# A fused attention and MLP kernel: the lower half of x behind the state update, chunks 8 to 11 in other places, and products of constants on TensorE among the first chunks

## The chip, the cores and the metric

The kernel runs on one core of a Trainium2 chip. The metric is the time of one execution on the device in microseconds; lower is better. The core's engines work side by side: TensorE (PE, with its weight loads shown apart as PEld), VectorE (DVE), ScalarE (ACT), GpSimd (POOL), and SyncE (SP), which here only issues DMA transfers. Every engine takes its instructions in the order in which the program lists them and waits for others through semaphores.

## The reference

Three layers in a row. The first is a linear attention with decay over blocks of 64 positions (batch 2, 8 heads, 768 positions, head size 64):

```python
for b in range(nb):
    intra = np.einsum('bhic,bhjc->bhij', qb, kb) * Dmask[None]
    intra = np.einsum('bhij,bhjd->bhid', intra, vb)
    inter = np.einsum('bhid,bhde->bhie', qb * lam_pow[None], kv_state)
    out[:, :, sl] = intra + inter
    kb_dec = kb * rev_pow[None]
    kv_state = lam_block[None, :, None, None] * kv_state + np.einsum('bhsd,bhse->bhde', kb_dec, vb)
```

Its output, 1536 tokens of 512 numbers, goes through `h = x @ w_in`, `g = max(0.01 h, h)`, `y = g @ w_out` (inner width 2048), and then through `((y @ w1) * (y @ w2)) @ w3 @ w_out` (width 1024).

## The kernel before

Tokens are worked in 12 chunks of 128 (two blocks of 64, all 8 heads); four chunks make a group of 512 tokens, three groups in all. Matrix products of the layers behind the attention are done with every float32 operand split into an upper and a lower half (a copy to `float32r` on ScalarE, and what is left by a subtraction on VectorE, line 161), three products for one.

`attention(n, rank, joined)` (line 350) lists the work of a chunk: two loads of 512 KB (q and k, then k and v; line 361), `k_decay` and `q_decay` (kd and qd), the front on TensorE (scores, then k times v for the new state; lines 369 to 381), the mask of the scores (line 384), for each of the two blocks a `fade` of the old state and an `update` (lines 441 to 462), and `outs`, the products of masked scores and of the state. Where `joined`, the outputs of the chunk before are laid between the products of this chunk's front in one operation (`scores`, line 420; recorded at line 429); this text calls such an operation a pass. `outputs` (line 513) issues the outputs of a group's last chunk alone (line 519). `done` (line 495) takes an output x from PSUM: `x_hi` on ScalarE, then the lower half on VectorE. The products of the attention are float32, 64 by 64 with 64 columns; two of them, or four in a pass, use different quarters of the array at once.

`unit_h` (line 556) makes one 128-wide piece of h for a group (12 products, line 530), `unit_y` (line 600) adds its share to y (12 products, line 537). They alternate; the first eight weight tiles serve all three groups before the next block of tiles is begun. Weights come as 64-bit numbers and are made float32 by ScalarE and VectorE (`convert`, line 213). All weight loads past the eighth stand in the program behind the outputs of chunk 7 (line 262).

The order of all this is not written out: `in_order` (line 64) simulates the engines with a cost for each operation in ns and, whenever an engine is free, lists the ready operation of the lowest `rank`. An operation is ready when what it comes `after` is done and its buffers are free; `behind` only asks that another has been listed. `RINGS` gives the number of buffers of each kind; those in `FIXED` are handed out in the order in which the program creates them. `PLACE` says which chunks load into `yf0`, `yf1`, `yf2` (memory that later holds y) instead of the two `inp` buffers; `CHUNKS` says beside which step k of the main loop a chunk is listed, with rank 100 + 20 k and a bit.

Of the kernel before, what the change touches and what calls it, by code (L numbers as in the profile page):

```python
# [14 lines left out]
P = 128  # L15
B, H, S, D = 2, 8, 768, 64
# [6 lines left out]
CPG = T // CH  # L23
# [99 lines left out]
def tile_kernel(ctx: ExitStack, tc, qkv, lamb, w_in, w_out, w1, w2, w3t, wo, out):  # L123
    nc = tc.nc
# [18 lines left out]
    def op(*args, **kwargs):  # L143
        o = Op(*args, **kwargs)
        ops.append(o)
        return o
# [3 lines left out]
    def new(buf, shape, dtype=F32):  # L150
        tags = TAGS.get(buf.ring, (buf.ring,))
        turn[buf.ring] = turn.get(buf.ring, -1) + 1
        buf.tile = pools[buf.ring].tile(shape, dtype, tag=tags[turn[buf.ring] % len(tags)], name=buf.ring)
        return buf.tile
# [4 lines left out]
    def lo(dst, hi_, src):  # L159
        def fn(e):  # L160
            engines[e].tensor_tensor(out=dst(), in0=src(), in1=hi_().bitcast(F32), op=ALU.subtract)  # L161
        return fn


    T_ = {}
# [170 lines left out]
    wo_buf, wo_first, wo_part = {}, {}, {}  # L336

    xs, x_ops = {}, {}
    st_op, x_done = {}, {}
    half = [slice(0, D), slice(D, P)]
    pend, turns = {}, []
# [4 lines left out]
    def attention(n, rank, joined):  # L350

        inp, a, qd, kd = Buf(PLACE.get(n, "inp")), Buf("a"), Buf("qd"), Buf("kd")
        sc, st = Buf("ps"), Buf("ps")
# [64 lines left out]
        back = pend.pop(n - 1) if joined else None  # L418

        def scores(e):  # L420
# [10 lines left out]
        fr = op(  # L431
            {"pe": 2100}, scores, rank, [*ld, k_op, *(back["after"] if back else [])],
            [sc, st, *(back["takes"] if back else [])], [inp, kd, *(back["uses"] if back else [])],
            behind=turns[-1:],
        )
        turns.append(fr)
        if back:
            back["done"](fr)
        masked = op({"dve": 660}, mask, rank, [fr, tables[0]], [a], [sc])

        def fade(k, c):
# [14 lines left out]
        def update(k, c, old):  # L456
            def fn(e):
                if old:
                    nc.vector.tensor_tensor(out=state(k), in0=st.tile[:, c], in1=T_["faded", c], op=ALU.add)
                else:  # L460
                    nc.vector.tensor_copy(state(k), st.tile[:, c])
            return fn

        for c in range(2 if carry else 1):
            k = 2 * n + c
# [3 lines left out]
                fo = op({"dve": 420} if early else {"act": 1000, "dve": 420, "pool": 700}, fade(k, c), rank + 0.4, [st_op[k], tables[1]], port=True)  # L469
            st_op[k + 1] = op({"dve": 420}, update(k + 1, c, old), rank + 0.5, [fr, fo, x_done.get(n - 2)], [], [st])  # L470

        g, c0 = divmod(n, CPG)
        px = Buf("acc" if early else "ps")
        if c0 == 0:
# [17 lines left out]
                            else:  # L492
                                yield o, state(2 * n + c)[h, p, :], qd.tile[h, p, c, :], False

        def done(xo):
            part = lambda v: xs[g].tile[:, v, :, c0 * CH : (c0 + 1) * CH]
            src = lambda: px.tile.rearrange("q p c i -> q p (c i)")
            r = xo.rank + 0.8

            def x_hi(e):  # L500
                nc.scalar.copy(part(0), src())  # L501

            o1 = op({"act": 580}, x_hi, r, [xo], [], [px, xs[g]])
            o2 = op({"dve": 660}, lo(lambda: part(1), lambda: part(0), src), r, [o1], [], [px, xs[g]])
            x_ops[g] += [o1, o2]
            x_done[n] = xo

        pend[n] = {
            "mms": outs, "done": done, "takes": [px, xs[g]] if c0 == 0 else [px], "uses": [inp, a, qd],
            "after": [masked, q_op, *([st_op[2 * n]] if inter else []), st_op[2 * n + 1]],  # L510
        }

    def outputs(n, rank):

        back = pend.pop(n)

        def fn(e):
            for o, w, mv, start in back["mms"]():
                nc.tensor.matmul(o, w, mv, start=start, stop=True, skip_group_check=True)

        xo = op({"pe": 2000}, fn, rank, back["after"], back["takes"], back["uses"], behind=turns[-1:])
        turns.append(xo)
        back["done"](xo)
# [32 lines left out]
    def unit_h(g, f, rank, rank_next):  # L556
        w, w_ops, wb = weight("in", f, g, rank)
        ps = Buf("ps")

        def mm(e):  # L560
            x = xs[g].tile
            full(new(ps, [P, T]), w, lambda b, cc: x[:, b, cc, :])

        def leaky(e):

            nc.scalar.activation(out=ps.tile, in_=ps.tile, func=AF.Prelu, alpha=0.01)  # L566

        o0 = op({"pe": 2720}, mm, rank, [*w_ops, *x_ops[g]], [ps], [wb, xs[g]], behind=last_h[-1:])
        last_h.append(o0)
        o1 = op({"act": 560}, leaky, rank_next, [o0], [], [ps])  # L570
        gp[g, f] = pair_ops(o1, ps, rank_next)
# [28 lines left out]
    def unit_y(g, f, rank):  # L600
        w, w_ops, wb = weight("out", f, g, rank)
        gb, g_ops = gp.pop((g, f))
        job = lambda c: (lambda v: w(v)[:, c * P : (c + 1) * P], lambda v: gb.tile[:, v, :])

        def evac(c, acc, o):
            if f < FB:
                def fn(e):
                    if c == 0:
                        yf[g] = const.tile([P, NCC, T], F32, tag=f"yf{g}", name=f"yf{g}")
                    nc.scalar.copy(yf[g][:, c, :], acc.tile)  # L610
                yf_ops[g, c] = op(
                    {"act": 560}, fn, rank + 1, [o, *([yf_ops[g, 0]] if c else [])], [] if c else [Buf(f"yf{g}")], [acc]
                )
            else:
                def fn(e):
                    nc.vector.tensor_tensor(out=yf[g][:, c, :], in0=acc.tile, in1=yf[g][:, c, :], op=ALU.add)
                yf_ops[g, c] = op({"dve": 660}, fn, rank + 1, [o, yf_ops[g, c]], [], [acc])
            if f == NF1 - 1:
                y_split(g, c, rank + 2)

        accumulate("y", g, f, FB, rank, [*w_ops, *g_ops], [wb, gb], job, EXACT, evac)
# [91 lines left out]


    consts = op({"dve": 100}, dve_consts, 0)
    lam_op = op({"q": 100}, load_lam, 0)
    pc = op({"pool": 600}, pool_consts, 0)
    tables = [
        op({"dve": 900}, table("dm", "w34_6", 0.0, lambda: T_["ident"][:, 0, :]), 0, [lam_op, pc]),
        op({"dve": 900}, table("lpow", "w34_7", 1.0, lambda: T_["zero"]), 1, [lam_op, pc]),  # L720
    ]
    PLACE = {0: "yf0", 1: "yf1", 2: "yf2", 5: "yf1", 6: "yf2", 9: "yf2"}
    for n in range(CPG):
        attention(n, 10 * n, n > 0)
    outputs(CPG - 1, 10 * CPG)
    rank = 100

    steps = [(g, f) for b in range(0, NF1, FB) for g in range(NG) for f in range(b, b + FB)]
    r = lambda k: rank + 20 * k
    CHUNKS = {0: (4, 5), 1: (6, 7), 2: (8,), 4: (9, 10), 5: (11,)}  # L730
    for k in range(2):
        unit_h(*steps[k], r(k - 2) + 10, r(k))
    for k, (g, f) in enumerate(steps):
        unit_y(g, f, r(k))
        for i, n in enumerate(CHUNKS.get(k, ())):
            attention(n, r(k) + 1 + 5 * i, n % CPG > 0)
            if n % CPG == CPG - 1:
                outputs(n, r(k) + 8)
        if k + 2 < len(steps):
            unit_h(*steps[k + 2], r(k) + 10, r(k + 2))  # L740
        if k >= len(steps) - 2 * NF2 and k % 2 == 0:
            wo_ops.extend(weight("wo", (k - len(steps) + 2 * NF2) // 2, 0, r(k) + 15)[1])
    rank = r(len(steps))
# [3 lines left out]
    for g in range(NG):  # L747
        r = lambda f: rank + 40 * f
# [7 lines left out]
        rank = r(NF2)  # L756
# [57 lines left out]
```

## Time and profile before

| | before |
|---|---|
| median of 3 runs | 560.65 us (560.33 to 561.94) |
| the profiled execution | 561.43 us |
| its span, first to last instruction | 559.7 us |
| TensorE busy | 540.2 us (97%) |
| VectorE busy | 316.0 us (56%) |
| ScalarE busy | 304.0 us (54%) |
| GpSimd busy | 68.9 us (12%) |
| moved by DMA | 54.07 MB, mean 97 GB/s |

All rows come from one profiled execution. Busy time of an engine says little by itself: what counts is where the engine that bounds a stage stands still, and what ended that. The timeline gives it in brackets behind an instruction: idle time before it, and the releaser. "issue" means that nothing in the profile explains the wait. The sums by stage give for each engine the busy time and, in brackets with an x, how many instruction records began there.

### The profile page before, as it was taken

How to read it: one execution, taken by the hardware profiler on the slowest of the kernel's cores; microseconds unless marked ns; L12 is line 12 of the kernel's file. 1: busy time of each engine (PE TensorE's matmuls, PEld its weight loads, DVE VectorE, ACT ScalarE, POOL GpSimd, SP SyncE). 2: the span in 40 equal slices, each digit the busy share in tenths (PEclk: the TensorE clock that was granted, in tenths of full speed). 3: DMA queues.
4: the chain of work that ended last, by engine and by line, in shares of the span. 5: the costliest groups of instructions: out<-in, count | busy, mean ns of one | idle time of the engine just before them, and what ended most of it. 6: DMA issues, size and time to landing. Idle time of an engine off the chain costs nothing.

```text
span 559.7 us, 9050 instructions
## 1 busy us (share of the span) xinstructions
PE 540.2 (97%) x3680; PEld 448.6 (80%) x3680; DVE 316.0 (56%) x519; ACT 304.0 (54%) x548; POOL 68.9 (12%) x60
## 2 busy tenths in 40 slices
PE   5699998999999999999999999999999999999997
PEld 4588886888888888888888888888888888888885
DVE  4797589781338951699816778884223333333331
ACT  4786797882228752486815666763334333343332
POOL 0033132000000000010101201110002111120110
PEclk9799999999999999999999999999999999999999
DMA  8971874541003440145501324420002000020002
GB/s 302 368 274 40 278 254 153 185 152 37 1 0 113 150 153 0 39 147 184 196 1 37 114 76 152 150 77 0 1 0 76 1 1 0 2 75 0 1 0 77
DMA packets 15738, 54.07 MB, mean 97 GB/s; under 512 B 1872, under 2 KB 1872, under 8 KB 15696
## 3 DMA queue, kind: packets, MB, share of 16 engines
q1 hardware_dynamic: 15696, 53.49, 27.5%
q8 instruction: 29, 0.48, 0.3%
q14 instruction: 13, 0.11, 0.1%
HBM read 50.33 MB, written 3.15 MB: 96 GB/s over the span
## 4 chain that ended last, share of the span: by engine, by line
PE 88%; ACT 4%; DMA 4%; DVE 2%; issue 1%; SPq 1%; ACTq 0%
PE ps L530 45%; PE acc L537 33%; PE ps L655 8%; DMA yf<-in_qkv_dram 2%; PE ps L429 1%; DMA inp<-in_qkv_dram 1%; PE acc L429 1%; ACT rn L235 1%; ACT rp L235 1%; ACT faded L447 1%; SPq L361 1%; ACT kd L399 0%; DVE f L254 0%; DVE rp L239 0%; ACT yf L610 0%
## 5 line engine op out<-in xcount | busy, mean ns | idle before, releaser
L530 PE MATMUL ps<-xy,wp 128*128 128x512 f32 x756 | 179.1, 389 | 0.0
L530 PEld LDWEIGHTS ps<-xy,wp 128*128 128x128 f32 x756 | 141.9, 188 | 29.6
L530 PE MATMUL ps<-xy,wa 128*128 128x512 f32 x396 | 95.3, 390 | 1.4 <-ACT xy L501 1.3
L537 PE MATMUL acc<-act,wa 128*128 128x512 f32 x396 | 96.1, 391 | 0.3 <-DVE act L161 0.3
L530 PEld LDWEIGHTS ps<-xy,wa 128*128 128x128 f32 x396 | 74.0, 188 | 17.3 <-ACT xy L501 1.4
L537 PEld LDWEIGHTS acc<-act,wa 128*128 128x128 f32 x396 | 73.9, 188 | 16.1 <-DVE act L161 0.7
L161 DVE TENSOR_TENSOR act<-ps,act 128x512 fp32r<-128x512 f32 x72 | 49.5, 687 | 60.2 <-ACT act L545 60.2
L537 PE MATMUL acc<-wp,act 128*128 128x512 f32 x288 | 69.0, 389 | 0.0
L235 ACT ACTIVATE rp<-raw,bp 128x512 f32<-128x512 uint16 x72 | 54.9, 766 | 19.1 <-DVE f L254 17.3
L157 ACT CAST wp<-wa 128x512 fp32r<-128x512 f32 x48 | 29.8, 622 | 64.5 <-PE ps L530 39.2
L537 PEld LDWEIGHTS acc<-wp,act 128*128 128x128 f32 x288 | 54.1, 188 | 11.2
L235 ACT ACTIVATE rn<-raw,bn 128x512 f32<-128x512 uint16 x72 | 54.5, 762 | 9.9 <-DVE rp L239 3.6
L566 ACT ACTIVATE ps<-ps 128x512 f32<-128x512 f32 x48 | 27.8, 580 | 56.5 <-PE ps L530 56.5
L239 DVE SCALAR_TENSOR_TENSOR rp<-rp,rn 128x512 uint32<-128x512 f32 x72 | 53.0, 737 | 5.2 <-ACT rp L235 3.9
L161 DVE TENSOR_TENSOR wp<-wa,wp 128x512 fp32r<-128x512 f32 x36 | 24.9, 691 | 49.9 <-ACT wp L157 49.9
L545 ACT CAST act<-ps 128x512 fp32r<-128x512 f32 x72 | 42.0, 583 | 5.8 <-DVE ps L691 3.1
L537 PE MATMUL acc<-act,wp 128*128 128x512 f32 x180 | 43.4, 390 | 0.0
L254 DVE SCALAR_TENSOR_TENSOR f<-rp,u 128x512 uint32<-128x512 uint32 x56 | 42.5, 765 | 0.4
L537 PEld LDWEIGHTS acc<-act,wp 128*128 128x128 f32 x180 | 33.7, 188 | 7.0
L245 DVE TENSOR_SCALAR u<-raw 128x512 uint32<-128x512 uint32 x72 | 31.6, 440 | 6.6 <-DMA raw<-in_w_in_dram 5.4
L691 DVE TENSOR_TENSOR ps<-ps,ta 128x512 f32<-128x512 f32 x24 | 16.8, 700 | 29.4 <-PE ps L530 29.4
L157 ACT CAST wp<-w 128x512 fp32r<-128x512 f32 x24 | 14.9, 621 | 32.3 <-PE ps L530 21.3
(87 smaller groups left out, 534.3 us busy)
## 6 DMA issues: line engine op xcount, KB each, us to landing
raw<-in_w_in_dram SPq DMA_DIRECT2D x16, 512.0 KB, 5.1
raw<-in_w_out_dram SPq DMA_DIRECT2D x16, 512.0 KB, 4.5
raw<-in_w3t_dram SPq DMA_DIRECT2D x16, 512.0 KB, 4.0
raw<-in_w_dram SPq DMA_DIRECT2D x16, 512.0 KB, 3.5
yf<-in_qkv_dram SPq DMA_DIRECT2D x12, 512.0 KB, 5.8
inp<-in_qkv_dram SPq DMA_DIRECT2D x12, 512.0 KB, 6.9
raw<-in_wo_dram SPq DMA_DIRECT2D x8, 512.0 KB, 4.2
out_dram<-f SPq DMA_DIRECT2D x12, 256.0 KB, 2.0
```

Source lines behind the costliest of these rows:

```text
L157: return lambda e: nc.scalar.copy(dst(), src())
L161: engines[e].tensor_tensor(out=dst(), in0=src(), in1=hi_().bitcast(F32), op=ALU.subtract)
L235: nc.scalar.activation(out=new(buf, [P, 512]), in_=top, func=AF.Relu, scale=8.0, bias=T_[bias])
L239: nc.vector.scalar_tensor_tensor(out=rp.tile.bitcast(U32), in0=rp.tile, scalar=32768.0, in1=rn.tile, op0=ALU.min, op1=ALU.add)
L245: nc.vector.tensor_scalar(out=new(u, [P, 512], U32), in0=mid, scalar1=2.0**-13, scalar2=2.0**19 - 1, op0=ALU.mult, op1=ALU.min)
L254: nc.vector.scalar_tensor_tensor(out=get().bitcast(U32), in0=rp.tile.bitcast(U32), scalar=16, in1=u.tile, op0=ALU.logical_shift_left, op1= ...
L530: nc.tensor.matmul(o, w(a)[:, cc * P : (cc + 1) * P], x(b, cc), start=k == 0, stop=k == 3 * NCC - 1)
L537: nc.tensor.matmul(o, st(a), mv(b), start=first and k == 0, stop=last and k == 2)
L545: nc.scalar.copy(buf.tile[:, 0, :], ps.tile)
L566: nc.scalar.activation(out=ps.tile, in_=ps.tile, func=AF.Prelu, alpha=0.01)
L655: nc.tensor.matmul(ps.tile, w(a)[:, k * P : (k + 1) * P], wo_part[j](b), start=j == 0 and n == 0, stop=j == NF2 - 1 and n == 2,)
L691: lambda e: nc.vector.tensor_tensor(out=pb.tile, in0=pb.tile, in1=ta.tile, op=ALU.mult),
```

## The change

Three edits, all in what is listed and in which order; no result is computed in another way. `done` is called after the updates of the next chunk are listed, and the lower half of x of chunk n-1 is put `behind` the first state update of chunk n. Chunk 8 loads into `yf1`; chunk 9 goes from step 4 to the end of step 3, chunk 10 stays beside step 4 and chunk 11 beside step 5, and the last outputs are listed five ranks earlier. And `keep_warm` lists products of two constant tiles (the identity as weights, zeros as 64 columns) into an accumulator that nobody reads: 26 ahead of everything, 8 behind the front of each of the first four chunks. With them the small load of lambda goes behind the first half-load of chunk 0.

```diff
+    def keep_warm(n, rank, behind=()):
+        buf = Buf("acc")
+
+        def fn(e):
+            o = new(buf, [P, D])
+            for _ in range(n):
+                nc.tensor.matmul(o, T_["ident"].rearrange("q c i -> q (c i)"), T_["zero"], start=True, stop=True)
+
+        return op({"pe": 115 * n}, fn, rank, [pc], [buf], behind=behind)
...
         turns.append(fr)
-        if back:
-            back["done"](fr)
         masked = op({"dve": 660}, mask, rank, [fr, tables[0]], [a], [sc])
...
             st_op[k + 1] = op({"dve": 420}, update(k + 1, c, old), rank + 0.5, [fr, fo, x_done.get(n - 2)], [], [st])
 
+        if back:
+            back["done"](fr, [st_op[2 * n + 1]])
...
-        def done(xo):
+        def done(xo, behind=()):
...
-            o2 = op({"dve": 660}, lo(lambda: part(1), lambda: part(0), src), r, [o1], [], [px, xs[g]])
+            o2 = op({"dve": 660}, lo(lambda: part(1), lambda: part(0), src), r, [o1], [], [px, xs[g]], behind)
...
-    lam_op = op({"q": 100}, load_lam, 0)
+    lam_op = op({"q": 400}, load_lam, 0.5)
...
-    PLACE = {0: "yf0", 1: "yf1", 2: "yf2", 5: "yf1", 6: "yf2", 9: "yf2"}
+    PLACE = {0: "yf0", 1: "yf1", 2: "yf2", 5: "yf1", 6: "yf2", 8: "yf1", 9: "yf2"}
     for n in range(CPG):
+        if n == 0:
+            keep_warm(26, -1)
         attention(n, 10 * n, n > 0)
+        keep_warm(8, 10 * n + 0.1, turns[-1:])
...
-    CHUNKS = {0: (4, 5), 1: (6, 7), 2: (8,), 4: (9, 10), 5: (11,)}
+    CHUNKS = {0: {4: 1, 5: 6}, 1: {6: 1, 7: 6}, 2: {8: 1}, 3: {9: 11}, 4: {10: 6}, 5: {11: 1}}
...
-        for i, n in enumerate(CHUNKS.get(k, ())):
-            attention(n, r(k) + 1 + 5 * i, n % CPG > 0)
+        for n, d in CHUNKS.get(k, {}).items():
+            attention(n, r(k) + d, n % CPG > 0)
             if n % CPG == CPG - 1:
-                outputs(n, r(k) + 8)
+                outputs(n, r(k) + d + 2)
```

## Rows read from the trace of the kernel before

**Rows 1.** The page: its first line, and the instruction queue (packets, MB, share).
```profile
span 559.7 us, 9050 instructions
...
q8 instruction: 29, 0.48, 0.3%
```

**Rows 2.** Busy us of PE, PEld, DVE, ACT, POOL; clock, DMA share, GB/s, by stage.
```profile
0.00:31.10 31.10, 18.38 (x561) 17.67 (x561) 19.86 (x46) 18.43 (x41) 4.92 (x11) 0.89 0.89 328
31.10:87.00 55.90, 55.90 (x917) 46.65 (x917) 42.58 (x71) 44.57 (x102) 16.89 (x14) 1.00 0.60 205
87.00:99.00 12.00, 9.25 (x196) 6.95 (x195) 11.40 (x23) 10.71 (x23) 0.00 (x0) 1.00 0.55 172
99.00:555.60 456.60, 456.60 (x2012) 377.32 (x2010) 242.11 (x382) 229.70 (x383) 47.13 (x36) 1.00 0.19 64
```

**Rows 3.** Timeline of TensorE: start, us, instruction, count, idle time before it and its releaser.
```profile
5.86 1.97 PE L429 MATMUL ps<-yf 64*64 64x64 f32 x32 [5.86 <-DMA yf<-in_qkv_dram]
...
16.04 0.37 PE L429 MATMUL acc<-qd,state 64*64 64x64 f32 x1 [1.08 <-issue]
...
22.60 0.37 PE L429 MATMUL acc<-qd,state 64*64 64x64 f32 x2 [3.12 <-issue]
...
26.94 0.33 PE L519 MATMUL acc<-qd,state 64*64 64x64 f32 x4 [0.33 <-DVE state L459]
...
28.61 0.27 PE L519 MATMUL acc<-qd,state 64*64 64x64 f32 x3 [1.23 <-issue]
```

**Rows 4.** Sums from the start to the last three pauses of rows 3 that instructions end.
```profile
0.00:14.96 14.96, 7.99 (x222) 7.72 (x222) 7.85 (x23) 7.33 (x17) 1.11 (x8) 1.00 0.85 308
0.00:19.47 19.47, 11.42 (x349) 11.01 (x349) 10.87 (x29) 9.39 (x23) 1.11 (x8) 0.91 0.89 333
0.00:27.39 27.39, 15.89 (x476) 15.25 (x477) 16.15 (x39) 15.73 (x37) 2.38 (x9) 0.88 0.91 337
```

**Rows 5.** Queues in the 0.05 us from 13.65, 20.20, 26.10 and 29.85: a packet begins.
```profile
q8 instruction: 1, 0.02, 117.5%
...
q8 instruction: 1, 0.02, 134.0%
...
q8 instruction: 1, 0.02, 122.2%
...
q8 instruction: 1, 0.02, 120.1%
```

**Rows 6.** Sums of two stretches inside joined passes, at either granted clock.
```profile
23.00:25.00 2.00, 2.00 (x81) 2.00 (x75) 1.02 (x2) 0.74 (x3) 0.00 (x0) 0.50 1.01 369
47.18:49.21 2.03, 2.03 (x130) 1.96 (x129) 2.00 (x2) 0.11 (x1) 1.27 (x1) 1.00 0.00 0
```

**Rows 7.** The page's costliest groups: weight loads of the long products, count, busy, mean ns.
```profile
L530 PEld LDWEIGHTS ps<-xy,wp 128*128 128x128 f32 x756 | 141.9, 188 | 29.6
```

**Rows 8.** Timeline of POOL's last constant and of ScalarE's first kd.
```profile
1.54 0.32 POOL L181 TENSOR_TENSOR ident<-ident 128x64 f32<-128x64 f32 x1
...
7.16 0.98 ACT L399 ACTIVATE kd<-yf,dm 128x128 f32<-128x128 f32 x3 [4.86 <-DMA yf<-in_qkv_dram]
```

**Rows 9.** Timeline of SyncE's queue: loads of chunk 5 and of chunk 11.
```profile
18.51 0.80 SPq L361 DMA_DIRECT2D yf<-in_qkv_dram  x2
...
77.59 1.62 SPq L361 DMA_DIRECT2D inp<-in_qkv_dram  x2
```

**Rows 10.** Timeline of VectorE: lower half of chunk 1's x, then the state.
```profile
19.30 0.69 DVE L161 TENSOR_TENSOR xy<-acc,xy 128x512 fp32r<-128x512 f32 x1 [1.48 <-ACT xy L501]
...
19.91 0.41 DVE L459 TENSOR_TENSOR state<-ps,faded 128x256 f32<-128x256 f32 x1
```

**Rows 11.** Timeline of TensorE from 87 us: first instruction behind each of three pauses.
```profile
88.08 0.50 PE L537 MATMUL acc<-act,wa 128*128 128x512 f32 x1 [0.30 <-DVE act L161]
...
93.95 0.33 PE L519 MATMUL ps<-a,inp 64*64 64x64 f32 x4 [1.06 <-DVE a L384]
...
97.30 0.49 PE L530 MATMUL ps<-xy,wa 128*128 128x512 f32 x1 [1.27 <-ACT xy L501]
```

## The prediction

> **What bounds the kernel now.** I read the page first, then the sums by stage, then the timeline of TensorE wherever a stage left it idle, and last the queues behind those pauses. The profiled execution's span is 559.7 us [rows 1]. The sums by stage show that TensorE never pauses from 31.1 to 87 us and from 99 to 555.6 us [rows 2]; the work in those stretches is the same after the change, so only three places can give or take time: the first 31.1 us (18.38 busy, 12.72 idle), the 12 us from 87 (9.25 busy, 2.75 idle), and the 4.1 us of last outputs, which the change doesn't touch.
>
> In the first stage the timeline shows what ended each pause [rows 3]: 5.86 us for the first load, 0.33 us for a state of VectorE, and three pauses of 1.08, 3.12 and 1.23 us in the middle of a run of products, whose releaser is "issue", so no semaphore. Counting TensorE's records (weight loads and products) up to those three gives 222+222 = 444, 349+349 = 698 and 476+477 = 953 [rows 4]: steps of 254 and 255. The instruction queue moved 0.48 MB in 29 packets [rows 1], 16.6 KB each. Three such packets begin at 13.65, 20.20 and 26.10 us [rows 5], each 2.4 to 2.5 us before one of the three pauses ends (16.04, 22.60, 28.61). So I read these pauses as waits for instructions: one block is about 255 records; entering a block asks for the next. Block 1 is entered at record 188 (444 less 256), about 10.2 us; its successor arrives at 16.04, 5.8 us later; the next two take 6.6 and 6.0 us from entry to arrival. A fourth packet begins at 29.85 [rows 5], 1.24 us after entry at 28.61, when the data queues were less full: 3.6 us in all with the same 2.4. The DMA engines were 0.89 busy over this stage [rows 2].
>
> This chain, 10.2 to 16.04 to 22.60 to 28.61, sets the end of the first four chunks; the last outputs of chunk 3 end at 29.2 us, chunk 4's front fills TensorE to 31.1, and the uninterrupted run starts. A pass with the front of one chunk and the outputs of the one before is 256 records.
>
> The trace agrees on the block with the Trainium skill (Runtime: NRT & Kernel Launch, section Instruction fetch mechanics), which has blocks of 16 KiB or 256 instructions, but the page calls the cost of a boundary mostly hidden. Here 5.43 us of pauses lie on it. By the page the added products would cost only their own time, a rival below.
>
> **The change, part by part.**
>
> *The products of constants.* One statement of float32 with 64 columns leaves two products and two weight loads here: the first front's 16 score statements stand as x32 [rows 3]. So 26 statements are 104 records, and 8 are 32; with four sets the stream up to chunk 3's outputs grows by 104 + 4 x 32 = 232 records, nine tenths of a block.
>
> Their duration isn't in the trace: a whole-array product with only 64 columns doesn't occur. A joined pass, whose products use a quarter of the array each, four at once, ran 130 records in 2.03 us at a granted clock of 1.00 and 81 in 2.00 us at 0.50 [rows 6]: 15.6 and 24.7 ns, so four quarters take 0.062 or 0.099 us. That is the lower bound for a whole-array product. The upper one is the 128x128 weight load of 188 ns [rows 7], if it isn't hidden. So 26 statements, 52 products, take 3.2 to 9.8 us; I take 0.1 us each, 5.2 us, because the passes are the nearest in columns and TensorE starts from idle. They start when POOL's last constant is done (1.54 + 0.32 = 1.86 us) [rows 8] and end at 7.1 (5.1 to 11.7). A set of 8 takes 1.0 to 3.0 us; I take 1.6 at the low clock, 1.0 at the high one.
>
> Before, the first front started at 5.86. Now it starts at 7.1, but its second half needs kd, which ScalarE begins at 7.16 when the second half of the load lands [rows 8], so little is lost.
>
> Now the boundaries, in records, by the old numbers 188, 444, 698, 953, 1209. The order becomes: products to 104, front 0 to 232, products 264, pass 1 488, products 520, pass 2 776, products 808, pass 3 1064, products 1096, outputs of chunk 3 1224. Before, those outputs ended at 992.
> - Block 1 is entered 84 records into front 0, at about 8.2 us (7.1 plus some 1.1 of front), 2 us earlier than before.
> - Block 2 arrives 5.8 us later, 14.0. Pass 1 stops 44 records before its end and waits for it from about 11.7.
> - Block 3 arrives 5.9 us on, 19.9. Meanwhile TensorE does 44 records, 8 products and 178 records of pass 2, and stops again.
> - Block 4: pass 2 ends at about 20.9, not 18.2 as now, and with it chunk 1's buffer comes free, for which SyncE's queue waits to load chunk 5 (18.51 before [rows 9]) and two weight tiles behind it. From about 18 to 21 the data queues have nothing, so this block comes in the light 3.6 us, 23.5, before TensorE gets there: 78 records, 8 products and 145 records of pass 3, some 4.3 us, so entry at 24.2.
> - Block 5 is asked for at 24.2, when that load and the two tiles fill the queues: 5.7 us, 29.9. The outputs of chunk 3 reach the boundary at about 27.5, with 15 records to go, and wait.
> They end at 30.0 instead of 29.2: +0.8 us. The pause of 2.4 us is also between those that lowered the clock (after 3.12 us the rate was that of 0.50 [rows 3, 6]) and the one that didn't (after 1.23 us chunk 4's front ran at full pace); chunk 4's front, two products at a time, takes about 1.6 us longer at the low clock (x32 in 1.97 us at the start [rows 3], twice that for its 64 against the 2 us it took), taken at half: +0.8. **First stage: +1.6 us.** Ends: block 5 in time gives outputs at 27.7, so -1.5; a slow price of the products gives +6.1 (both below).
>
> *Lower half behind the state.* In chunk 1 VectorE idled 1.48 us for ScalarE's upper half, then did the lower half at 19.30 and the state only at 19.91 [rows 10]; the state now takes that gap. TensorE was waiting for instructions until 22.60, so this buys nothing there; for chunk 3 it removes the 0.33 us wait [rows 3], which lies inside the block chain too. The lower half comes 0.34 us later and holds its accumulator longer, but the buffer is taken again only four takes later. Zero both ways; if the instruction waits went, it would be worth 0.3.
>
> *The lambda load* goes behind chunk 0's first half-load on SyncE, which so starts sooner, under the products. The two tables on VectorE then wait for data that queue behind that half-load. They are wanted at 7.16, when the second half lands [rows 8]; at worst they come with it and their scans push kd, and the entry of block 1, by 1 us. I take zero of 0 to +1, since the first half has landed by 5.86 [rows 3].
>
> *Chunks 8 to 11.* Chunk 8 moves to yf1, so its two loads wait for chunk 5's outputs (about 49 us, not 38.75) but are wanted only at 60; the inp buffers pass to chunks 10 and 11 one turn sooner. Chunk 11's load, issued at 77.59 because its buffer was chunk 8's [rows 9], can go when chunk 7's outputs end, about 62. Chunk 9's pass comes before the fifth weight unit instead of behind it. On SyncE these loads then stand ahead of weight tiles of the next block of units, which comes only after the third group's. In the trace the pauses behind 87 us come from chunk 11 being late: 1.06 us for its masked scores and 1.27 for its x, and 0.30 for a half-result that VectorE did late, behind chunk 11's kd [rows 11]. With chunks 9 to 11 done one unit pair earlier, h of the third group has everything. VectorE and ScalarE are busy 42.58 and 44.57 of 55.9 us before [rows 2], so the moved work has room. **-2.6 us** (ends: 0 and -2.75).
>
> **Sum:** +1.6 - 2.6 = -1.0 us. The profiled execution took 561.43 us (span 559.7 and 1.73 around it); that gives 560.4. The median of the runs, 560.65, is 0.8 below it; by the median 559.6.
>
> **The rivals.**
> - *Block 5 in time.* If the data queues are light at 24 us too, outputs end at 27.7, h starts 1.5 us earlier: -1.5 - 2.6 = -4.1, 556.5 us. For it: the fourth packet waited only 1.24 us with data moving. Against: at 22.60, 4 us behind chunk 5's load, it waited 3.5.
> - *The first products outlast the load (slower).* Place: TensorE before front 0. At 188 ns each they end at 11.7, and all that follows shifts by 4.5: +6.1 - 2.6 = +3.5, 564.1 us. It turns the sign where a product costs over 0.12 us (1 us later per 0.019), and passes 0.3% above 0.15. For it: no row excludes that a weight load is exposed beside 64 columns; against: in the main loop it is hidden.
> - *The clock alone decides.* If blocks don't bind, the recorded clock of 0.89 over 31.1 us [rows 2] says 3.4 us were lost: -3.4 - 2.6 = -6.0, 554.6 us. Against: the three packets. The Trainium skill (TensorE: Matmul & The Clock Gate, Part 1) says activity releases a throttled clock, which is what such products would rest on.
> - *The chunks move but the pause stays*, behind another late weight or half-result: +1.6, 562.2 us.
>
> **How the numbers follow.** About 0.3%, 1.7 us, is what a measurement can tell. My forecast has 0.43 (own range 558.0 to 561.6): 0.13 faster, 0.28 same, 0.02 slower. Block 5 in time 0.25, faster. Products outlasting 0.18: 0.15 slower, 0.03 same. Clock alone 0.06, faster. Pause stays 0.08: 0.05 same, 0.03 slower. Together faster 0.44, same 0.36, slower 0.20. The range runs from 555.8 to 563.6; it leaves out the clock case (0.06), the slow case above 563.6 (0.11) and small tails (0.03).
>
> **What would show it.** Instruction packets near 11.6, 17.5, 21 and 27.5 us, with TensorE idle up to 2.4 us behind each; chunk 3's outputs ending near 30; no pause over 0.3 us from 87 to 99. I am wrong if no "issue" pause stands before 31 us, if the first front starts past 9 us, or if chunk 11's masked scores are waited for again.

## The result and the profile after

The changed kernel is slower: 565.87 us median of four runs against 560.49 of four, a ratio of 1.0082 (95% interval 1.0059 to 1.0105). The forecast was 559.6 us, with a range of 555.8 to 563.6. The profiled execution was the longest of the four, 567.5 us with a span of 565.7, 6.0 more than the span before; the medians differ by 5.4.

The sums by stage (columns as in [rows 2]) are cut where the same things happen as before: up to the first products of h, the stretch without a pause behind them, the stretch with chunk 11, the rest.

```profile
0.00:39.25 39.25, 33.72 (x677) 32.71 (x677) 21.13 (x48) 18.80 (x42) 5.09 (x11) 0.96 0.75 268
39.25:81.50 42.25, 42.25 (x739) 35.33 (x738) 32.12 (x56) 32.48 (x76) 6.11 (x5) 1.00 0.62 223
81.50:105.00 23.50, 22.95 (x375) 18.36 (x374) 22.67 (x40) 20.44 (x39) 5.42 (x5) 1.00 0.45 156
105.00:561.50 456.50, 456.50 (x2012) 377.34 (x2010) 241.20 (x381) 230.12 (x384) 47.53 (x36) 1.00 0.19 65
```

Against [rows 2], the first stage is 39.25 us instead of 31.1: +8.15. The pauses around chunk 11 are 0.55 us instead of 2.75: -2.2. The long rest is 456.5 instead of 456.6. Together that is 5.85 of the 6.0 us. The whole loss lies ahead of h, where TensorE's idle time fell from 12.72 to 5.53 us while its busy time rose from 18.38 to 33.72.

TensorE's timeline shows what filled it. These rows answer to [rows 3] and, the last, to [rows 11]:

```profile
1.91 11.36 PE L345 MATMUL acc<-zero,ident 128*128 128x64 f32 x52 [1.91 <-POOL ident L181]
...
16.23 2.00 PE L345 MATMUL acc<-zero,ident 128*128 128x64 f32 x16
...
19.96 0.21 PE L440 MATMUL ps<-yf,kd 64*64 64x64 f32 x1 [0.20 <-issue]
...
35.74 0.27 PE L530 MATMUL acc<-a,inp 64*64 64x64 f32 x2 [3.42 <-issue]
...
82.98 0.50 PE L541 MATMUL ps<-xy,wa 128*128 128x512 f32 x1 [0.50 <-DVE a L395]
```

The 52 products of constants take 11.36 us, 0.218 us each, and hold the first front until 13.2 us, 7.3 later than in [rows 3]. Each of the four sets of 16 takes 2.0 us. So products cost 11.4 + 8.0 = 19.4 us of TensorE's time. The other work ahead of h took 33.7 - 19.4 = 14.3 us instead of 18.4: 4.1 us came back, the clock being up from about 15.5 to 32.3 us, without the low stretches between the pauses of the kernel before. Pauses shrank by 7.2 us. 19.4 - 4.1 - 7.2 gives the 8.1.

The pauses of 1.91, 0.20 and 3.42 us are all of the 5.53 us: from 1.91 us to the start of h, TensorE waits for no other engine and for no data. A shift in the order of the other engines' work is therefore not what holds it up in this stage.

Instruction blocks are still in sight. The sums up to the last pause and the queue's half microsecond from 33.0:

```profile
0.00:32.31 32.31, 30.20 (x604) 29.32 (x605) 17.71 (x43) 13.79 (x32) 3.17 (x10) 1.00 0.76 275
```

```profile
q8 instruction: 1, 0.02, 12.7%
```

604 + 605 = 1209 records, the next step after the 444, 698 and 953 of [rows 4], and the packet is again 2.2 to 2.7 us ahead of the end of the pause. That boundary is 15 records short of the end of chunk 3's outputs. At 444 records only 0.20 us is left of a pause, at 698 and 953 nothing: with the products in the stream TensorE comes to these boundaries later than the blocks do. Behind the 3.42 us the clock is low again: the 3.51 us from there to h run at 0.53 on the mean.

### The profile page after: what moved, and what is told of

Same layout as the page of the kernel before. It is cut to its first block, busy times and chain, and to the rows that moved or that the text cites. A ratio compares the mean times of both kernels' runs of the same rounds, so it can differ in the third digit from the quotient of the medians.

```text
span 565.7 us, 9269 instructions
## 1 busy us (share of the span) xinstructions
PE 555.6 (98%) x3796; PEld 463.7 (82%) x3796; DVE 317.1 (56%) x524; ACT 302.5 (53%) x540; POOL 64.2 (11%) x57
## 4 chain that ended last, share of the span: by engine, by line
PE 94%; DMA 2%; DVE 2%; issue 1%; ACT 1%; POOL 0%; SPq 0%; POOLq 0%
PE ps L541 45%; PE acc L548 33%; PE ps L666 8%; PE acc L345 3%; PE ps L440 3%; DMA raw<-in_w_out_dram 1%; DMA yf<-in_qkv_dram 1%; DVE f L254 0%; PE acc L530 0%; PE ps L530 0%; DVE wa L161 0%; DVE rp L239 0%; PE acc L440 0%; DVE a L395 0%; ACT faded L456 0%
## 5 line engine op out<-in xcount | busy, mean ns | idle before, releaser
L548 PEld LDWEIGHTS acc<-act,wa 128*128 128x128 f32 x396 | 74.0, 188 | 15.5
L254 DVE SCALAR_TENSOR_TENSOR f<-rp,u 128x512 uint32<-128x512 uint32 x56 | 39.6, 713 | 0.5
L157 ACT CAST wp<-w 128x512 fp32r<-128x512 f32 x24 | 14.9, 622 | 32.3 <-PE ps L541 21.0
```

The costliest lines, as they stand in the source:

```text
L157: return lambda e: nc.scalar.copy(dst(), src())
L254: nc.vector.scalar_tensor_tensor(out=get().bitcast(U32), in0=rp.tile.bitcast(U32), scalar=16, in1=u.tile, op0=ALU.logical_shift_left, op1= ...
L548: nc.tensor.matmul(o, st(a), mv(b), start=first and k == 0, stop=last and k == 2)
```

## The experiments

The idle time from 60 to 105 us in this table is TensorE's, from the sums of each run's profile; h is where its first product for h starts (line 530 before, 541 in the change). Ratios are to the kernel before on the same chip.

| run | ratio (95%) | h starts, us | idle 60 to 105, us |
|---|---|---|---|
| the kernel before | 1 | 31.0 | 2.75 |
| the change | 1.0082 (1.0059 to 1.0105) | 39.25 | 0.55 |
| e1 no products | 0.9973 (0.9958 to 0.9988) | 32.6 | 1.2 |
| e2 and lambda first | 0.9964 (0.9947 to 0.9981) | 30.3 | 0.8 |
| e3 sets only | 1.0119 (1.0100 to 1.0138) | 39.8 | 1.2 |
| e4 first 26 only | 1.0058 (1.0042 to 1.0073) | 36.0 | 0.6 |
| e5 chunks only | 0.9985 (0.9968 to 1.0002) | 32.9 | 1.35 |
| e6 state only | 1.0014 (0.9997 to 1.0032) | 30.9 | 3.35 |
| e7 sets of few records | 1.0052 (1.0028 to 1.0077) | 37.7 | 1.2 |
| e8 non-zero columns | 1.0078 (1.0052 to 1.0103) | 35.85 | 0.3 |
| e10 later loads | 0.9974 (0.9953 to 0.9994) | 30.5 | 0.6 |
| e11 first 8, on e2 | 0.9982 (0.9965 to 0.9999) | 31.0 | 0.6 |
| e12 first long, on e2 | 0.9976 (0.9957 to 0.9995) | 32.3 | 0.5 |

A ratio rests on 4 to 12 runs, the two columns behind it on one profile each, and where h starts differs from execution to execution. The change and e8 have the same records on TensorE and, by the runs, the same time, but e8's profile has h 3.4 us earlier: its wait at record 1209 was 1.51 us instead of 3.42, and no low clock came behind it.

```profile
33.81 0.27 PE L530 MATMUL acc<-a,inp 64*64 64x64 f32 x2 [1.51 <-issue]
```

### Are the products the loss?

**e1**, the changed kernel without them:

```diff
-        if n == 0:
-            keep_warm(26, -1)
...
-        keep_warm(8, 10 * n + 0.1, turns[-1:])
```

> The changed kernel without any product of constants; the order of the state, the chunks and the lambda load stay changed. Theory: the whole loss is the products. In the changed kernel the first 52 end at 13.3 us instead of the 7.1 I took, and the run of h starts at 39.25 us instead of 31.1. Without them the first front starts with its load, the blocks of instructions bind as before, and h starts near 32 (the lambda load behind the first half-load made kd wait until 8.3 us, 1.2 us later than before), while the pauses behind 81 us stay short (0.5 instead of 2.75). Sum +1 - 2.2: about 559.3 us, ratio to the kernel before 0.998. Rival: the moved loads or the later lower half cost something too; then over 562 us.

**e2**, in addition lambda as before:

```diff
-    lam_op = op({"q": 400}, load_lam, 0.5)
+    lam_op = op({"q": 100}, load_lam, 0)
```

> As e1, with the lambda load ahead of everything again. Theory: the small load of 128 rows of 16 bytes behind the first half-load holds up the loads behind it (from 4 to 6 us 199 GB/s moved against 317 before), so kd of chunk 0 goes back from 8.3 to 7.2 us and the whole chain with it: about 1 us less than e1, 558.3 us, ratio 0.996. Rival: the later start of the first loads in e1 has other causes and the block chain swallows it: same as e1 within 0.3 us.

Sums of the first stage and of the later one, e1 and then e2:

```profile
0.00:32.60 32.60, 19.30 (x561) 18.34 (x561) 20.54 (x48) 19.16 (x42) 4.68 (x11) 0.87 0.89 319
60.00:105.00 45.00, 43.78 (x695) 35.94 (x694) 36.53 (x64) 37.92 (x75) 7.57 (x7) 1.00 0.63 215
```

```profile
0.00:30.30 30.30, 17.50 (x561) 16.58 (x561) 19.89 (x46) 18.02 (x41) 4.65 (x11) 0.89 0.89 336
60.00:105.00 45.00, 44.20 (x654) 36.28 (x650) 37.67 (x65) 37.95 (x72) 7.27 (x6) 1.00 0.59 205
```

Both ratios came out as expected: without products the rest of the change is a gain of 0.27% and 0.36%, so the loss comes with the products. In e1 the front of chunk 0 starts at 5.11 us, but then stands 1.58 us for kd, because the tables, made from lambda, come at 5.35 us instead of 2.6; in e2 that pause isn't there. By the profiles e2's h comes 2.3 us before e1's; by the runs the two intervals overlap, so the price of lambda's place isn't shown by the times (559.78 and 559.39 us, close to the "same within 0.3 us" of e2's rival).

**e3** has only the sets, **e4** only the first 26 (each leaves out the other call of the diff above).

> The changed kernel without the 26 statements ahead of all; the four sets of 8 stay. Theory: 128 records more than e1 until chunk 3's outputs end, 1120 in all, which stays short of the boundary at 1209; each set takes 1.9 us (fast) to 3.5 us (slow), but one part of it lies in waits for instruction blocks. h starts near 34.5 us, total about 561.5 us. Rival (time alone: every set is on the path): four times 1.9 to 3.5 us more than e1, 567 us or more.

> The changed kernel with only the 26 statements ahead of all. Theory: the first front starts at 13.2 us as in the changed kernel, 7.3 us later than before; 104 records more, 1096 until chunk 3's outputs end, short of the boundary at 1209. But the data of chunks 0 to 4 have landed by 20 us, so blocks come in the light 3.6 us, and some of the lateness is won back: h near 33 to 35 us, total about 561 us. Rival (all of the lateness stays): e1 plus 7 us, 566 us.

Both misses, and in the same direction: 568.1 and 564.8 us instead of 561.5 and 561. e3's time is that of its rival, by which every set lies on the path; e4's lies between theory and rival. Against e1's 559.8 us the sets alone cost 8.3 us, the first 26 alone 5.0, and both together (by the ratios) about 6.1: the two prices don't add up, and e4 says that without its sets the change is still slower than before. In e3's timeline:

```profile
30.16 0.48 PE L440 MATMUL acc<-qd,state 64*64 64x64 f32 x4 [4.17 <-issue]
...
30.57 3.67 PE L345 MATMUL acc<-zero,ident 128*128 128x64 f32 x16
```

and its sums behind that set:

```profile
34.24:39.80 5.56, 5.56 (x129) 5.49 (x129) 1.65 (x4) 1.90 (x4) 1.28 (x1) 0.62 0.17 49
```

A pause of 4.17 us stands ahead of the fourth set, the set then takes 3.67 us instead of 2.0, as the first one did, and the 129 products behind it run at a mean granted clock of 0.62 and take 5.56 us. The set did not bring the clock back; it stood ahead of chunk 3's outputs and held them up. In the change the long pause came behind the fourth set. That is one reason for e3's later end by the profiles (566.9 us against 565.7); by the runs the two intervals just touch. In e4 the last pause was the longest too:

```profile
30.66 0.27 PE L440 MATMUL ps<-inp,kd 64*64 64x64 f32 x2 [4.31 <-issue]
```

The last block did not come in the light 3.6 us that I had counted on: with the start late, chunk 5's load and two weight tiles are issued from 22.0 (e3) and 22.2 us (e4) instead of 18.5 [rows 9], and the DMA engines are at 0.98 to 1.02 from 24 to 28 us, while that block is on its way.

### What do the other parts bring?

**e5** is the kernel before with the new `PLACE` and `CHUNKS`; **e6** the kernel before with this:

```diff
-        if back:
-            back["done"](fr)
...
+        if back:
+            back["done"](fr, [st_op[2 * n + 1]])
...
```

> The kernel before with nothing but the new places of chunks 8 to 11. Theory: h starts at 31.1 us as before; the pauses from 60 to 105 us, 2.75 us before, shrink to the 0.8 to 1.2 us that e1 and e2 had: about 1.7 us less, ratio 0.997. Rival: the gain of e2 came from the state's place, and this is 1.000.

> The kernel before with nothing but the lower half of x behind the state update. Theory: TensorE waits for instructions where it would gain, so no change that a measurement can tell: h between 30.5 and 31.2 us, pauses behind 87 us as before, ratio 0.9995 to 1.0005. Rival: this is where the gain of e2 comes from, ratio 0.997.

Their sums of the first stage and of 60 to 105 us, e5 and then e6:

```profile
0.00:32.95 32.95, 18.40 (x561) 17.69 (x561) 20.70 (x48) 19.12 (x42) 4.64 (x11) 0.90 0.87 317
60.00:105.00 45.00, 43.65 (x694) 35.88 (x693) 35.88 (x63) 37.89 (x76) 7.35 (x7) 1.00 0.63 215
```

```profile
0.00:30.90 30.90, 17.84 (x561) 16.87 (x561) 19.77 (x46) 18.03 (x41) 4.75 (x11) 0.83 0.88 327
60.00:105.00 45.00, 41.65 (x659) 33.72 (x655) 32.66 (x56) 36.51 (x78) 8.95 (x7) 1.00 0.66 221
```

e5's later pauses are 1.35 us instead of 2.75 and its ratio 0.9985; that its first stage is 1.8 us longer is mostly one pause for instructions of 4.50 instead of 3.12 us [rows 3], ahead of anything e5 changes on TensorE. So the profile agrees with the theory, but the ratio lies halfway between theory (0.997) and rival (1.000), and its interval takes in 1: the gain isn't shown by the times. e6 brings nothing that the runs can tell. e2's 0.9964 is somewhat better than the two together, and one profile of each doesn't say why.

### Do blocks of instructions end the pauses?

**e7** keeps each set's time but makes it of long products:

```diff
+            if n < 26:
+                o = new(buf, [P, 8, D])
+                for _ in range(n // 4):
+                    nc.tensor.matmul(
+                        o, T_["ident"].rearrange("q c i -> q (c i)"),
+                        T_["zero"].unsqueeze(1).to_broadcast([P, 8, D]), start=True, stop=True,
+                    )
+                return
```

> The changed kernel with each set of 8 statements of 64 columns replaced by 2 statements of 512 columns: 8 records instead of 32 for a similar time (4 products of 0.45 to 0.9 us, 1.9 to 3.6 us). Theory of instruction blocks: the outputs of chunk 3 end with record 1128 instead of 1224, short of the boundary at 1209, so the pause of 3.43 us that stood 15 records ahead of their end no longer holds up x; what is left of it falls into chunk 4's front. h at 36 to 37.5 instead of 39.25 us, ratio about 1.004. Rival (that pause was no wait for instructions): the pause stays in chunk 3's outputs and the ratio is 1.008.

A set, the sums up to the last pause, and the instruction behind that pause:

```profile
21.29 1.98 PE L346 MATMUL acc<-zero,ident 128*128 128x512 f32 x4
```

```profile
0.00:34.16 34.16, 32.25 (x604) 26.45 (x604) 18.91 (x44) 14.51 (x35) 4.39 (x11) 1.00 0.75 268
```

```profile
36.87 0.27 PE L448 MATMUL ps<-inp,kd 64*64 64x64 f32 x2 [2.71 <-ACT xy L520]
```

Three of the sets take the same 2.0 us, the first 2.54. The pause stands at 604 + 604 = 1208 records again, but that record now belongs to chunk 4's front, as expected; the profile names ScalarE as releaser there, but eight products with the same operands had run ahead of the pause. The position of the pause follows the count of records, not the operation: this is the plainest evidence for the blocks. The gain is less plain. h starts 1.5 us earlier, at 37.7 us just behind the 36 to 37.5 that were expected, but the low clock behind the pause now falls on the first products of h (0.62 on the mean from 37.7 to 42.2 us). The ratio is 1.0052, and its interval overlaps that of the change.

**e10** tried to shorten the wait for a block by queueing less data ahead of it:

```diff
-EARLY = [15, 35, 35]
+EARLY = [15, 102.5, 102.6]
...
-    PLACE = {0: "yf0", 1: "yf1", 2: "yf2", 5: "yf1", 6: "yf2", 8: "yf1", 9: "yf2"}
+    PLACE = {0: "yf0", 1: "yf1", 2: "yf2", 4: "yf0", 5: "yf1", 6: "yf2", 8: "yf1", 9: "yf2"}
```

> e2 with chunk 4 loading into yf0 (so its load waits for chunk 0's outputs at 12.8 us) and the second and third weight tile behind it on the queue. Theory: an instruction packet waits 3.4 to 4.2 us because the data queues are full up to 20 us; with 2 MB fewer ahead of it the first packet comes near 12.8 instead of 13.7 us, the next near 18.5 instead of 19.7, and the run of h starts 1 to 2 us before the 30.3 of e2: ratio about 0.994. Rival (the wait of a packet doesn't hang on how much data is queued): packets and h as in e2, or later because chunk 4 comes late: 0.996 or more.

```profile
15.92 0.27 PE L440 MATMUL acc<-qd,state 64*64 64x64 f32 x1 [0.91 <-issue]
...
22.09 0.37 PE L440 MATMUL acc<-qd,state 64*64 64x64 f32 x2 [3.75 <-issue]
...
28.11 0.27 PE L530 MATMUL acc<-qd,state 64*64 64x64 f32 x3 [1.72 <-issue]
```

The pauses end within 0.5 us of those of e2 (16.04, 22.21 and 27.68 us), and the ratio is 0.9974: that is what the rival said. It is no proof against the queues: the DMA engines' share of this stage was 0.93, so they were as full as ever, only in another order. For them speaks the changed kernel: the packets near 21 and 25 us came within 2 us of the boundary that asks for them (records 444 and 698, at 19.6 and 23.9 us), while the DMA share was 0.54 from 20 to 22 us and 0.15 or less from 22 to 26, and their blocks cost no pause. The one at 33 us came nearly 6 us after its boundary (record 953, at 27.6 us), with shares of 0.90 to 0.99. But in e8 the same packet came near 31.4 us, 3.9 us after that boundary, at shares of 0.79 to 1.01. That full queues lengthen the wait is likely by these rows; what sets its length isn't shown.

### What does a product of constants cost, and what does it do for the clock?

**e8** takes other data for the columns:

```diff
-                nc.tensor.matmul(o, T_["ident"].rearrange("q c i -> q (c i)"), T_["zero"], start=True, stop=True)
+                nc.tensor.matmul(o, T_["ident"].rearrange("q c i -> q (c i)"), T_["ident"][:, 1, :], start=True, stop=True)
```

> The changed kernel with columns of the identity in place of the zeros as moving operand. Theory (the rate hangs on the form of the product, not on its data): the first 52 products stay at 0.218 us each and end at 13.3 us, ratio 1.008. Rival (products of zeros leave the clock low, others raise it): the rate goes to 0.12 us on the way, the first set ends at 8 to 10 us, and the ratio is 1.000 to 1.004.

```profile
1.91 11.35 PE L345 MATMUL acc<-ident 128*128 128x64 f32 x52 [1.91 <-POOL ident L181]
```

The data make no difference to the price nor to the clock in this stretch: 11.35 us at the same rate from end to end.

**e9** replaces the 26 by four forms of 6 statements, without sets; it is a measurement, run once (565.39 us):

```diff
+            for count, weights, cols in ((6, full, 64), (6, full[:, 0:64], 64), (6, full, 128), (6, full, 512)):
```

> A measurement, not a version: the changed kernel without its four sets, and ahead of all, in place of the 26 statements, four times 6 statements (12 products each): 128-wide weights with 64 columns, 64-wide weights with 64 columns, 128-wide with 128 columns, 128-wide with 512 columns. Theory (weight load and columns run one after the other, each about 0.107 us at the low clock): 0.218, 0.165, 0.32 and 0.96 us a product while the clock is low. And the long ones raise the clock after some us, which 11.4 us of 64-column products did not: the last group goes to 0.45 us on the way. Rival (the weight load is hidden and the columns alone cost): 0.218, 0.218, 0.43, 1.7. Rival on the clock: no product of constants raises it; the last group keeps its price to the end.

Groups by form, busy time and mean ns of one (a mean holds the overlap of neighbours, so the price is busy time over 12):

```profile
L351 PE MATMUL acc<-zero,ident 128*128 128x512 f32 x12 | 5.3, 592 | 0.0
L351 PE MATMUL acc<-zero,ident 128*128 128x64 f32 x12 | 2.8, 426 | 1.9 <-POOL ident L181 1.9
L351 PE MATMUL acc<-zero,ident 128*128 128x128 f32 x12 | 2.4, 369 | 0.0
L351 PE MATMUL acc<-zero,ident 128*64 128x64 f32 x12 | 1.5, 319 | 0.0
```

0.23 us with 64 columns, 0.20 with twice as many, 0.125 with half-wide weights. The last group's 0.44 us is nearly e7's price at the high clock (1.98 us for four), so the clock had risen before it. The sums from the start show where (us, busy time and products begun, then clock, DMA share, GB/s):

```profile
0.00:4.80 4.80, 2.88 (x13) 1.00 0.45 122
0.00:6.00 6.00, 4.08 (x24) 1.00 0.56 159
0.00:6.80 6.80, 4.88 (x27) 1.00 0.62 181
0.00:7.60 7.60, 5.68 (x31) 1.00 0.64 196
0.00:8.40 8.40, 6.49 (x37) 1.00 0.68 215
```

With half-wide weights 11 products begin in 1.2 us, 0.11 us apart. With 128 columns 4 begin in 0.8 us, 0.20 apart, and then 6 in the next 0.8, the last of them the first long one: the rate rose from about 7.6 us on, before any product of 512 columns. Both theories fall: load and columns don't add up, and the columns alone aren't it. A product costs the longer of the two, and here the load of 128-wide float32 weights is no shorter than the columns up to 128 of them.

**e11** and **e12** put fewer products ahead of e2, in the time in which TensorE mostly waits for data anyway: `keep_warm(8, -1)`, and `keep_warm(3, -1)` with 512 columns as in e7.

> e2 with 8 statements of the product of constants ahead of all: 16 products of 0.218 us end at 5.4 us, ahead of the first data. Theory: they neither delay the first front nor raise the clock, and move the block boundaries by 32 records only: same as e2 within 0.6 us, ratio 0.996 to 0.9975. Rival (a head start for the clock is worth something where it is hidden): 1 us or more less than e2, under 0.995.

> e2 with 3 statements of 512 columns ahead of all: 6 products of some 0.9 us, from 1.9 to 7.3 us, 12 records. Theory: if long columns do raise the clock, front 0 and pass 1 run at the high rate from about 8 us; but front 0 waits for its load (kd at 7.2 us) and pass 1 for chunk 1's (about 10 us), and block 1 is entered at most 0.5 us earlier: same as e2 within 0.6 us, ratio 0.9955 to 0.9975. Rival (the clock bounds the first chunks): 2 us or more less than e2, 0.993 or under.

The long products of e12, and its first front:

```profile
1.92 5.49 PE L345 MATMUL acc<-zero,ident 128*128 128x512 f32 x6 [1.92 <-POOL ident L181]
...
7.33 1.19 PE L443 MATMUL ps<-yf 64*64 64x64 f32 x32
```

The six products take 0.9 us each to the end, twice the 0.44 of e9's long group: the rate was still the low one. They outlast the first load, so the front begins 1.3 us later than in e2 (6.06), but it takes 1.19 us instead of the 1.97 of [rows 3]. So the clock rose as the front began, and it is worth nothing that can be told: 0.9976, with h at 32.3, no better than e2 and not the 2 us of the rival. e11 is 0.9982; its 16 products end at 5.6 us, ahead of the first data, and gain nothing either. Both ratios lie a little above the ranges expected. For the first chunks, loads and instruction blocks are the bound, not the clock that the first front finds; what a clock held high through the later pauses would be worth, no run shows.

**e2 beats both kernels**: 0.9964 (0.9947 to 0.9981) of the kernel before, against 1.0082 for the change.

## Why the prediction was wrong

**The step that failed** is the first term of the sum: "I take 0.1 us each, 5.2 us", with the first set ending at 7.1 us. A product took 0.218 us, and the 52 ended at 13.27 us. That is above even the upper bound of 0.188: that row [rows 7] is a weight load of the high clock, beside products of 512 columns, and I let it bound a load at the low clock. The nearest in columns, the joined pass, was the wrong neighbour: its 64 by 64 weights are half as wide, and in e9 half-wide weights cost about half, 0.125 us against 0.23. With it fell the sets, 2.0 us each instead of 1.0 to 1.6.

**A second step failed with it: the sets were laid into waits for blocks.** In the forecast TensorE does 8 products and then "stops again", so that the sets cost nothing of their own. In the change those waits are gone (0.20 us at 444 records, nothing at 698 and 953), and the four sets' 8.0 us lie on TensorE's path. e3 shows it without the 26: the sets alone lose 8.3 us against e1.

**The likeliest case was the wrong one; the slower rival named the place, and its sum came close partly by luck.** It said that the first products outlast the load, that everything behind shifts with them, and that 0.15 us a product is enough for a loss that can be measured. Put in the measured end, 13.27 us, and its own rule gives +1.6 + (13.27 - 7.1) - 2.6 = +5.2 us; the medians moved by 5.4. It had 0.18, and its time ended at 564.1 because the price was bounded too low. But the shift is not handed on whole: in e4 the front starts 7.1 us later than in e2 (13.20 against 6.06) and h 5.7. And the waits that the rule leaves in place were gone, while 8.0 us of sets and a last wait of 3.42 stood in their stead. These errors nearly cancelled. (By its own ends, 11.7 and 7.1, the shift that it names is 4.6 us and not 4.5.)

**The blocks were right in place, not in weight.** The pause 15 records ahead of the end of chunk 3's outputs was foretold with 2.4 us and came with 3.42, at record 1209 (1.51 in e8). The arithmetic of records carried over to e7. The low clock behind that pause was priced at half of 1.6 us and came whole: 3.51 us from the pause to h, against 2.04 in e8 at the high clock. But the two waits foretold at 444 and 698 did not come: blocks no longer bound the stage, TensorE's own work did, 33.72 of 39.25 us. And from entry at record 953 (27.6 us) to going on at 35.74 the last block took 8.2 us instead of 5.7 (6.3 in e8). The reading of before also left out one wait, 1.10 us for masked scores, so that its five pauses make 11.62 of the 12.72 us idle:

```profile
14.05 0.27 PE L429 MATMUL acc<-a,yf 64*64 64x64 f32 x2 [1.10 <-DVE a L384]
```

**The signs.** Packets were foretold near 11.6, 17.5, 21 and 27.5 us; the trace has them near 17.5, 21, 25 and 33. Of the signs of being wrong one came in full: the first front started past 9 us. Of "issue" pauses before 31 us only the 0.20 is left. Chunk 11's masked scores were not waited for again.

**Chunks 8 to 11** were foretold at -2.6 us and brought -2.2 in the change's profile, -1.4 in e5's: the pauses behind chunk 11 went, and a smaller one for masked scores (0.50 us in the change, for those of chunk 9, and 1.27 in e5) came in their place, earlier. **The state's place** was foretold at zero, and the runs tell no difference (e6). **Lambda** was taken at zero of 0 to +1; in the change the products cover it, and in e1 TensorE waits 1.58 us for kd behind it.

**The clock** I had as a rival of its own, 3.4 us to win. The size came from a granted clock that reads 1.00 in the first stretch, where the pace is the low one, so it is no measure. The Trainium skill (TensorE: Matmul & The Clock Gate, Part 1) has activity release the clock; the trace doesn't agree for this form of product: 11.36 us in which TensorE is never idle left the rate at 0.218 us, and the first front behind them still started at its old pace, 1.97 us. In e9 and e12, with other forms, the rate had risen by 8.4 and 7.4 us. What tells these apart for the chip, no run here shows.

## What to carry to other kernels

Price a filler by its own form at the clock at which it will run: with few columns the weight load is the price, and a row from a stretch where the load is hidden doesn't bound it. Before filling an engine's idle time, ask whether the time is idle for want of that engine: here it stood for data and for instructions. Short fillers gained nothing (e11, e12), and those of the change cost 5.0 us (the 26 alone, e4) and 8.3 us (the sets alone, e3) against e1. Count instruction records in dense stretches of small products; here the pauses sat at fixed counts. And read a start time from one profile with care: here it moved by 3.4 us between two executions with the same records.

## What the runs showed of the hardware

- TensorE stands for instructions every 254 to 256 records when a block's packet is late: at 444, 698, 953 and 1209 records, whatever operation is there. A packet begins 2.2 to 2.7 us before the pause ends.
- A float32 product of 128-wide weights costs 0.22 us with 64 columns at the low clock and 0.125 at the high one; with 128 columns 0.20 at the low clock; with 64-wide weights and 64 columns 0.11 at the low clock (e9); with 512 columns 0.9 (e12) and 0.44 (e9).
- Under back-to-back products of 64 columns with 128-wide weights the rate stayed the low one for all of 11.4 us, with zeros or with columns of the identity (e8). In e9, where other forms followed after 2.7 us, it had risen before 8.4 us, under products of 128 columns; in e12, behind six products of 512, by 7.4 us.
- The 2 KB load of lambda, first on the queue, is used 1.8 us after its issue (0.80 to 2.60); behind one 512 KB load it takes 4.1 us (1.23 to 5.35 in e1).
- The granted clock reads 1.00 in the first 15 us of the change's profile, although the same product goes at 0.218 us there and at 0.125 later; ahead of the first change of the clock the pace is the better witness.
